# Routing logits from a stationary gate matrix, in pieces per batch, and Sinkhorn column sums set apart

## The chip, the cores and the metric

The program runs on one core of one Trainium2 chip. The metric is the device time of one execution in microseconds, the median of several runs. The engines are named as in the profile: PE is TensorE's matmul, PEld its weight load, DVE is VectorE, ACT is ScalarE, POOL is GpSimd and SP is SyncE, which here only issues DMAs.

## What is computed

Three stages follow each other. The weights and the attention inputs are float32.

```
attn = softmax(q @ k.T / 8 + causal mask + min(-(cum_i - cum_j), 0)) @ v     # 4 batches, 8 heads, 576 x 64
x    = elu(attn_tokens @ w_in) @ w_out                                       # 2304 x 512, 512 -> 2048 -> 512
logits = x @ w_gate                                                          # 2304 x 8
P = exp(logits - logits.max())
for _ in range(8):
    P /= P.sum(1, keepdims=True) + 1e-09
    P /= P.sum(0, keepdims=True) + 1e-09
    P *= N / E                                                               # N = 2304, E = 8
out = sum over e of P[:, e:e+1] * (relu(x @ w1[e]) @ w2[e])                  # 512 -> 1024 -> 512 for 8 experts
```

The change concerns the line with `w_gate` and the loop that normalizes P.

## The kernel before, in words

The first phase does attention and the first feed-forward stage together. Attention works on jobs of two heads: S tiles hold the scores (PE, L302), POOL makes the bias tiles R from the running sums (L273, L276), DVE adds them (L321), ACT takes the exponential (L329), POOL scales the rows (L337), PE transposes them (T, L364 to L370), ACT and DVE copy the transposes, and PE multiplies by V (X, L431). The feed-forward stage has groups of twelve matmuls: `m` groups (L677) for the first layer and `n` groups (L709) for the second. A weight decode for it runs on ACT and DVE (L614 to L634) from tiles `st` that SP loads (L581). The running sums come to `cum` tiles by SP's DMAs (L239), which copy a row to 64 partitions. Batch by batch the feed-forward result lies in `acc`, transposed: 128 of the 512 features on the partitions, four such quarters d, 576 tokens along the row.

When the eight pieces of a batch's `acc` are done, `gate(b)` (L776) makes its logits. It takes 128 tokens of one quarter d of `acc` as the stationary operand and the 128x8 quarter of the gate matrix as the moving one, and adds up four d in PSUM. A batch has four whole blocks of 128 tokens and one of 64, so these are 20 matmuls; a float32 matmul is two instructions in the trace, a pass each, so the trace has 40 for a batch. Two DVE copies (L797, L799) put the logits into `P_t`, a tile of 128 x 18 x 8.

The second phase is the mixture of experts, with `product` (L1006; banks A, B and C, L1023: seven products of six matmuls for each step) and `m2_l2` (L1078; `b`, L1092: twelve matmuls). While its first steps run, the Sinkhorn loop is fitted in: `max_t` and `max_b` bring the global maximum to all partitions, `rows()` divides by the row sums and leaves partial column sums in `small` (L833 to L837), and `cols(it)` multiplies these by a matrix of ones on PE (`col`, L844), after which DVE divides by them (L848 to L850) and calls `rows()` again. There are eight such rounds, and `m2_l2` of the second unit needs the result.

What sets the order: the Python code keeps a model clock `flow` (class `_Flow`, L50). Work for PE is emitted by `flow.pe(cost, fn)`, and what follows it on the other engines by `flow.after(dt, fn)`. `extras()` (L886) is called after each group of the second phase and emits the next Sinkhorn matmul if its input has been emitted. The sequence so emitted is the priority by which the framework's scheduler then lays each engine's instructions in a line, so an edit of one operation can move others. Each engine then runs its own line strictly in that order; PE alone loads the weights of later matmuls ahead. The gate's matrix `wg` is loaded at the start (L1145), the first POOL work are memsets and `make_identity` (L1147 to L1158).

## Time and profile before

| | us |
|---|---|
| runs shown | 2206.74, 2211.27, 2213.0 |
| their median | 2211.27 |
| the profiled execution's own time | 2213.01 |
| its span in the profile | 2211.2 |
| PE busy (share of the span) | 2151.1 (97%) |
| PEld busy | 1901.1 (86%) |
| DVE busy | 1294.1 (59%) |
| ACT busy | 940.2 (43%) |
| POOL busy | 823.3 (37%) |

Busy PE does not mean PE at its peak: matmuls overlap, and the clock granted to TensorE can stand at one of two levels, 1.2 or 2.4 GHz. The profile gives it as a share (PEclk): 1.00 is 2.4 GHz and 0.50 is 1.2 GHz. In the 40 slices of the span, PE is busy nine tenths or more in all but the first three, and PEclk is nine tenths or more in all but the first two, each slice a mean over 55 us.

### The profile page before, as it was taken

Reading aid. Unit: us, or ns where it says so; the run is one execution under the profiler, and the core shown is the slowest. Engines: PE = TensorE matmul, PEld = TensorE weight load, DVE = VectorE, ACT = ScalarE, POOL = GpSimd, SP = SyncE. Lnnn points to the kernel's source line nnn. Section 1 sums busy time; section 2 is a strip of 40 time slices with the busy share of each in tenths; the row PEclk is TensorE's granted clock in tenths of the full one; section 3 lists DMA queues with packets and bytes.
Section 4 is the critical chain, followed back from the end, with each engine's and each line's share of the span. In section 5 each row is a group of like instructions: output and inputs, shape, how many; then the busy total and the mean of one; then the engine's idle time right before and its main releaser. Section 6 shows DMA issues by size and latency. Waiting matters only on the chain.

```text
span 2211.2 us, 33504 instructions
## 1 busy us (share of the span) xinstructions
PE 2151.1 (97%) x12236; PEld 1901.1 (86%) x12236; DVE 1294.1 (59%) x2921; ACT 940.2 (43%) x2201; POOL 823.3 (37%) x1046
## 2 busy tenths in 40 slices
PE   6789999999999999999999999999999999999999
PEld 3357988999998898989998989989899899899898
DVE  5678698555756755555555555555555455555554
ACT  3565545343433444344434444343434443443432
POOL 5676343232402343333333343433333333434330
PEclk8899999999999999999999999999999999999999
DMA  6454444243562421222215221222115221222121
GB/s 198 154 167 169 145 169 159 79 131 106 188 229 96 150 77 59 66 77 67 67 58 195 77 77 58 67 68 76 65 60 195 77 70 56 76 67 77 58 67 38
DMA packets 102227, 228.55 MB, mean 103 GB/s; under 512 B 8816, under 2 KB 24688, under 8 KB 102064
## 3 DMA queue, kind: packets, MB, share of 16 engines
q1 hardware_dynamic: 97456, 209.65, 28.9%
q10 hardware_dynamic: 4608, 16.78, 1.9%
q8 instruction: 96, 1.57, 0.3%
q14 instruction: 67, 0.55, 0.1%
HBM read 189.10 MB, written 37.30 MB: 102 GB/s over the span
## 4 chain that ended last, share of the span: by engine, by line
PE 88%; DVE 5%; POOL 2%; DMA 1%; ACT 1%; issue 1%; SPq 0%; POOLq 0%; DVEq 0%; ACTq 0%
PE b L1092 36%; PE A L1023 18%; PE C L1023 9%; PE n L709 7%; PE m L677 7%; PE B L1023 5%; PE S L302 2%; PE X L431 2%; PE T L364 1%; PE gate L789 1%; DVE R L321 1%; POOL R L273 1%; DVE h L692 0%; DMA xr<-x_d 0%; DVE r L689 0%
## 5 line engine op out<-in xcount | busy, mean ns | idle before, releaser
L1092 PE MATMUL b<-w,h 128*128 128x512 f32 x3456 | 844.7, 393 | 0.0
L1092 PEld LDWEIGHTS b<-w,h 128*128 128x128 f32 x3456 | 645.5, 188 | 125.1
L906 POOL TENSOR_TENSOR w1c<-S,w1c 128x512 fp32r<-128x512 f32 x192 | 263.6, 1395 | 860.6 <-ACT w1c L905 860.6
L1023 PE MATMUL A<-xc,w1c 128*128 128x384 f32 x2304 | 449.5, 336 | 0.0
L1106 DVE SCALAR_TENSOR_TENSOR acc<-b,P_t,acc 128x512 f32<-128x512 f32 x264 | 197.5, 748 | 423.1 <-PE b L1092 423.1
L1023 PEld LDWEIGHTS A<-xc,w1c 128*128 128x128 f32 x2304 | 406.3, 188 | 7.8
L1036 ACT ACTIVATE h<-pre_P 128x384 fp32r<-128x384 f32 x288 | 151.4, 526 | 437.6 <-DVE pre_P L1049 437.3
L677 PE MATMUL m<-xT,w 128*128 128x288 f32 (+2 forms) x1536 | 231.3, 305 | 2.9 <-DVE r L689 1.5
L1023 PE MATMUL C<-xc,w1c 128*128 128x384 f32 x1152 | 233.9, 337 | 0.0
L709 PE MATMUL n<-h,w 128*128 128x288 f32 (+2 forms) x1536 | 222.3, 299 | 3.3 <-DVE r L689 1.6
L677 PEld LDWEIGHTS m<-xT,w 128*128 128x128 f32 x1536 | 214.2, 194 | 12.4 <-issue 5.0
L709 PEld LDWEIGHTS n<-h,w 128*128 128x128 f32 x1536 | 207.3, 188 | 17.3 <-issue 11.1
L1023 PEld LDWEIGHTS C<-xc,w1c 128*128 128x128 f32 x1152 | 206.0, 189 | 7.5
L906 DVE TENSOR_TENSOR w<-sw,w 128x512 fp32r<-128x512 f32 x192 | 155.5, 831 | 59.9 <-ACT w L905 59.9
L1039 DVE SCALAR_TENSOR_TENSOR h<-pre_P,h 128x384 fp32r<-128x384 f32 x288 | 160.8, 558 | 12.3 <-ACT h L1036 0.5
L273 POOL TENSOR_SCALAR R<-cum,cum_m 128x256 f32<-128x256 f32 (+4 forms) x144 | 101.8, 707 | 155.5 <-PE T L370 90.6
L337 POOL TENSOR_SCALAR R<-R,sm 128x64 f32<-128x64 f32 (+8 forms) x144 | 92.5, 650 | 118.6 <-DVE sm L334 64.0
L1036 ACT ACTIVATE h<-A 128x384 fp32r<-128x384 f32 x96 | 47.2, 491 | 192.8 <-PE A L1023 192.8
L905 ACT CAST w<-sw 128x512 fp32r<-128x512 f32 x192 | 109.4, 619 | 21.5 <-PE n L709 16.8
L1057 ACT COPY pre_P<-A 128x384 f32<-128x384 f32 x192 | 92.4, 481 | 60.1 <-PE A L1023 60.1
L1023 PE MATMUL B<-xc,w1c 128*128 128x384 f32 x576 | 117.5, 339 | 0.0
L1023 PEld LDWEIGHTS B<-xc,w1c 128*128 128x128 f32 x576 | 104.6, 190 | 7.8 <-issue 0.2
(162 smaller groups left out, 2288.2 us busy)
## 6 DMA issues: line engine op xcount, KB each, us to landing
sw<-in_w_dram SPq DMA_DIRECT2D x192, 512.0 KB, 3.3
w<-w_sc SPq DMA_DIRECT2D x56, 512.0 KB, 3.6
w_sc<-w ACTq DMA_DIRECT2D x32, 512.0 KB, 3.3
xc_d<-xs SPq DMA_DIRECT2D x28, 384.0 KB, 3.2
xc<-xc_d SPq DMA_DIRECT2D x14, 768.0 KB, 6.0
QK<-in_qk_dram SPq DMA_DIRECT2D x16, 576.0 KB, 5.1
st<-in_wi_dram SPq DMA_DIRECT2D x16, 512.0 KB, 4.5
st<-in_wo_dram SPq DMA_DIRECT2D x16, 512.0 KB, 4.0
```

The costliest lines, as they stand in the source:

```text
L273: nc.gpsimd.tensor_scalar(out=t[:, 0:w], in0=ct[j].rearrange("p w k -> p (w k)")[:, S * z : S * z + w], scalar1=8.0, scalar2=cum_m[:, z, m ...
L337: nc.gpsimd.tensor_scalar(out=R[:, 0:keys], in0=R[:, 0:keys], scalar1=sm[:, 5:6], scalar2=1.0, op0=ALU.mult, op1=ALU.mult)
L677: nc.tensor.matmul(ps[:, 0:n], t[:, a, d * P : (d + 1) * P], x[:, z, d, c0 : c0 + n], start=(d == 0 and o == 0), stop=(d == 3 and o == 2))
L709: nc.tensor.matmul(ps[:, 0:n], t[:, a, f * P : (f + 1) * P], h[:, z, c0 : c0 + n], start=(f == 0 and o == 0), stop=(f == 3 and o == 2))
L905: nc.scalar.copy(hi, x)
L906: eng.tensor_tensor(out=lo, in0=x, in1=f32(hi), op=ALU.subtract)
L1023: nc.tensor.matmul(ps, t[:, a, wi_, kt * P : (kt + 1) * P], x[:, z, kt], start=(first and kt == 0 and o == 0), stop=(kt == 1 and o == 2), ...
L1036: nc.scalar.activation(h[:, 0], src, AF.Relu)
L1039: nc.vector.scalar_tensor_tensor(out=h[:, 1], in0=src, scalar=0.0, in1=f32(h)[:, 0], op0=ALU.max, op1=ALU.subtract)
L1057: nc.scalar.copy(new(name), ps)
L1092: nc.tensor.matmul(ps, h[:, z, c0 : c0 + P], t[:, a, :], start=(f == 0 and o == 0), stop=(f == 3 and o == 2))
L1106: nc.vector.scalar_tensor_tensor(out=a, in0=ps, scalar=q, in1=a, op0=ALU.mult, op1=ALU.add)
```

## The change

The gate turns its operands round. The gate matrix, padded with zeros from 8 to 32 columns, becomes the stationary operand, and 256 or 320 tokens of `acc` stream past it. Quarter d of the features writes its 8 partial logits to PSUM partitions 32d and up, so four matmuls fill four column quarters of the array. ACT copies the 128 rows to the tile `lt`. A second product, `gate_sum`, has 128 tokens of `lt` as the stationary operand and the matrix `sel` (eight columns, which add rows 0 to 7 of the four quarters) as the moving one. A batch goes in two pieces, 256 and 320 tokens or the other way round; each piece is emitted one group of the loop after the other. POOL makes `sel` out of the identity and clears `wg` at the start; the load of `wg` moves behind the first weight load. Finally `rows()` notes a time, model clock plus 3.0, before which `extras()` emits no further column sum. Lines from 149 on are two higher in the changed file, and from the gate on some 22 to 32 higher.

```diff
--- before.py
+++ after.py
@@ -109,6 +109,7 @@
     RA = 9
     NR, NQK, NCB, NSCAN, NA_T, NH = 5, 2, 2, 1, 1, 5
     NX = 3
+    SINKGAP = 3.0
 
 
 
@@ -148,7 +149,8 @@
         "rs": cst.tile([P, 18], F32, tag="rs", name="rs"),
         "cs": cst.tile([P, E], F32, tag="cs", name="cs"),
         "small": cst.tile([P, 16], F32, tag="small", name="small"),
-        "wg": cst.tile([P, 4, E], F32, tag="wg", name="wg"),
+        "wg": cst.tile([P, 4, 32], F32, tag="wg", name="wg"),
+        "sel": cst.tile([P, E], F32, tag="sel", name="sel"),
     }
 
 
@@ -725,7 +727,7 @@
                 nc.sync.dma_start(x2_d[:, d, t0 : t0 + n], a)
                 x2[b] = x2.get(b, 0) + 1
                 if x2[b] == 8:
-                    gates.append(b)
+                    gates.append((gate, b, 0))
 
             flow.after(12 * _mm(n) + 0.05, ev)
         return fn
@@ -774,31 +776,50 @@
     last_g = {k: max(g for g in range(GA) if groups[g][3][1] == k) for k in range(NCHUNK)}
 
 
-    def gate(b):
-
+
+
+    def gate(b, z):
         x, wg_t = accs[b], phc["wg"]
-        ps = ps_s.tile([P, 512], F32, tag="S", name=f"gate{b}")
-        parts, t0 = [], b * S
-        while t0 < (b + 1) * S:
+        cut = [0, 256 + 64 * (b % 2), S]
+        c0, n = cut[z], cut[z + 1] - cut[z]
+        lt = mo1.tile([P, 320], F32, tag="lt", name=f"lt{b}_{z}", bufs=1)
+        ps = ps_s.tile([P, 512], F32, tag="S", name=f"gate{b}_{z}")
+        for d in range(4):
+            nc.tensor.matmul(ps[32 * d : 32 * d + 32, 0:n], wg_t[:, d, :], x[:, d, c0 : c0 + n],
+                             start=True, stop=True)
+
+        def ev():
+            nc.scalar.copy(lt[:, 0:n], ps[:, 0:n])
+            gates.append((gate_sum, b, z, lt, c0, n))
+
+        flow.after(1.1, ev)
+
+    def gate_sum(b, z, lt, c0, n):
+        ps = ps_s.tile([P, 512], F32, tag="S", name=f"gs{b}_{z}")
+        parts, t0 = [], b * S + c0
+        while t0 < b * S + c0 + n:
             r0 = t0 % P
-            n = min(P - r0, (b + 1) * S - t0)
-            parts.append((t0 // P, r0, n, t0 - b * S))
-            t0 += n
-        for i, (tt, r0, n, c0) in enumerate(parts):
-            for d in range(4):
-                nc.tensor.matmul(ps[r0 : r0 + n, 8 * i : 8 * i + 8], x[:, d, c0 : c0 + n], wg_t[:, d, :],
-                                 start=(d == 0), stop=(d == 3))
+            m = min(P - r0, b * S + c0 + n - t0)
+            parts.append((t0 // P, r0, m, t0 - b * S - c0))
+            t0 += m
+        for i, (tt, r0, m, at) in enumerate(parts):
+            nc.tensor.matmul(ps[r0 : r0 + m, 8 * i : 8 * i + 8], lt[:, at : at + m], phc["sel"],
+                             start=True, stop=True)
+        if z == 0:
+            gates.append((gate, b, 1))
         whole = [i for i, x in enumerate(parts) if x[2] == P]
-        half = next(i for i, x in enumerate(parts) if x[2] < P)
+        half = [i for i, x in enumerate(parts) if x[2] < P]
 
         def ev():
             L = phc["P"]
-            i, tt = whole[0], parts[whole[0]][0]
-            nc.vector.tensor_copy(L[:, tt : tt + 4, :], ps[:, 8 * i : 8 * i + 32].rearrange("p (t e) -> p t e", t=4))
-            tt, r0, n, _ = parts[half]
-            nc.vector.tensor_copy(L[r0 : r0 + n, tt, :], ps[r0 : r0 + n, 8 * half : 8 * half + 8])
-            phc["logits"] = phc.get("logits", 0) + 1
-        flow.after(0.2, ev)
+            i, tt, k = whole[0], parts[whole[0]][0], len(whole)
+            nc.vector.tensor_copy(L[:, tt : tt + k, :],
+                                  ps[:, 8 * i : 8 * i + 8 * k].rearrange("p (t e) -> p t e", t=k))
+            for i in half:
+                tt, r0, m, _ = parts[i]
+                nc.vector.tensor_copy(L[r0 : r0 + m, tt, :], ps[r0 : r0 + m, 8 * i : 8 * i + 8])
+            phc["logits"] = phc.get("logits", 0) + z
+        flow.after(0.8, ev)
 
     def logits():
         L, small = phc["P"], phc["small"]
@@ -836,6 +857,7 @@
         nc.vector.tensor_tensor(out=L, in0=L, in1=rs.unsqueeze(2).to_broadcast([P, 18, E]), op=ALU.mult)
         nc.vector.tensor_reduce(out=small[:, 8:16], in_=L.rearrange("p t e -> p e t"), axis=AX.X, op=ALU.add)
         phc["step"] += 1
+        phc["due"] = flow.now + SINKGAP
 
     def cols(it):
         def fn():
@@ -862,7 +884,7 @@
     extra += [(lambda it=it: phc.get("step") == 3 + it, 0.1, cols(it)) for it in range(SINK)]
 
     def extras(force=False):
-        while extra and (force or extra[0][0]()):
+        while extra and (force or (extra[0][0]() and flow.now >= phc.get("due", 0.0))):
             ready, cost, fn = extra.pop(0)
             flow.until(ready)
             flow.pe(cost, fn)
@@ -1142,9 +1164,9 @@
         "r (m z q) -> r m z q", z=2, q=64)
     nc.sync.dma_start(s_raw, s)
     qk_load(0)
-    nc.sync.dma_start(phc["wg"], wg)
     nc.vector.memset(ones, 1.0)
     make_identity(nc, ident)
+    nc.gpsimd.memset(phc["wg"], 0.0)
     nc.gpsimd.memset(mask, 0.0)
     for z in range(2):
         nc.gpsimd.affine_select(
@@ -1183,12 +1205,22 @@
     for i in set_r[0]:
         r_step(i)
     w_dma()
+    nc.sync.dma_start(phc["wg"][:, :, 0:E], wg)
+    sel = phc["sel"]
+    nc.gpsimd.tensor_tensor(out=sel, in0=ident[:, 0:E], in1=ident[:, 32 : 32 + E], op=ALU.add)
+    for i in (64, 96):
+        nc.gpsimd.tensor_tensor(out=sel, in0=sel, in1=ident[:, i : i + E], op=ALU.add)
 
     def att_wait():
         t = att_next_ready()
         if t > flow.now:
             flow.flush(t)
             flow.now = t
+
+    def gates_run():
+        while gates:
+            fn, *args = gates.pop(0)
+            flow.pe(1.0, lambda: fn(*args))
 
     def att_end(k):
         return apos["n"] > chunk_last[k]
@@ -1236,14 +1268,14 @@
                 s_load()
             if "w" in m2 and g in (m2["w"] + 24, m2["w"] + 32):
                 w1_prep(int(g > m2["w"] + 24), 0.0)
-        while gates:
-            flow.pe(2.5, lambda: gate(gates.pop(0)))
+        gates_run()
         w_advance(g)
         flow.until(lambda: all(w in w_done for w in ws) and x_left[k[1]] == 0)
         flow.pe(cost, fn)
     flow.drain()
     while gates:
-        flow.pe(2.5, lambda: gate(gates.pop(0)))
+        gates_run()
+        flow.drain()
     pools["xp%d" % ((B - 1) % NX)].release()
     pools["mo1"].release()
     pools["dec"].release()
```

The order of the instructions moves at the places below. In each name the letters and the first numbers are the tile's, the last number is a buffer's.

The first is the start, on the queue of SP, which issues the loads, from `cum1` on; `st` are weights for the decode, `cum` the running sums, `V` and `QK` inputs of attention. Before:

```order
L239 DMA cum1_137<-cum_d_95 64x256 x2
L581 DMA st0_169<-in_wi_dram 128x1024
L581 DMA st1_171<-in_wi_dram 128x1024
L239 DMA cum2_185<-cum_d_95 64x256 x2
L210 DMA QK2_207<-in_qk_dram 128x2x256
L239 DMA cum3_234<-cum_d_95 64x256 x2
L210 DMA QK3_272<-in_qk_dram 128x2x256
L239 DMA cum4_330<-cum_d_95 64x576 x2
L581 DMA st2_315<-in_wi_dram 128x1024
L239 DMA cum4_330<-cum_d_95 64x512 x2
```

In the changed kernel:

```order
L583 DMA st0_170<-in_wi_dram 128x1024
L241 DMA cum1_138<-cum_d_95 64x256 x2
L583 DMA st1_172<-in_wi_dram 128x1024
L1208 DMA wg_102<-in_wg_dram 128x4x8
L241 DMA cum2_190<-cum_d_95 64x256 x2
L212 DMA QK2_212<-in_qk_dram 128x2x256
L241 DMA cum3_239<-cum_d_95 64x256 x2
L212 DMA QK3_277<-in_qk_dram 128x2x256
L583 DMA st2_320<-in_wi_dram 128x1024
L241 DMA cum4_335<-cum_d_95 64x576 x2
```

`st0` now stands ahead of `cum1`, and `st2` ahead of both loads of `cum4`. On POOL, in the same stretch, the scalings of R2 and R4 (`sm` is the factor) stood ahead of the bias tiles R8 to R11, which need `cum2`. Before:

```order
L337 TENSOR_SCALAR R0_164<-R0_164,sm1_179 128x128
L337 TENSOR_SCALAR R2_180<-R2_180,sm2_200 128x192
L337 TENSOR_SCALAR R2_180<-R2_180,sm3_201 128x256
L337 TENSOR_SCALAR R4_202<-R4_202,sm4_227 128x64
L337 TENSOR_SCALAR R4_202<-R4_202,sm5_228 128x128
L273 TENSOR_SCALAR R8_267<-cum2_185,cum_m_103 128x128 x2
L276 TENSOR_TENSOR R8_267<-R8_267,mask_104 128x64
L273 TENSOR_SCALAR R10_325<-cum2_185,cum_m_103 128x256
L276 TENSOR_TENSOR R8_267<-R8_267,mask_104 128x64
L273 TENSOR_SCALAR R10_325<-cum2_185,cum_m_103 128x256
L276 TENSOR_TENSOR R10_325<-R10_325,mask_104 128x64 x2
```

In the changed kernel:

```order
L275 TENSOR_SCALAR R8_272<-cum2_190,cum_m_104 128x128 x2
L278 TENSOR_TENSOR R8_272<-R8_272,mask_105 128x64
L275 TENSOR_SCALAR R10_330<-cum2_190,cum_m_104 128x256
L278 TENSOR_TENSOR R8_272<-R8_272,mask_105 128x64
L275 TENSOR_SCALAR R10_330<-cum2_190,cum_m_104 128x256
L278 TENSOR_TENSOR R10_330<-R10_330,mask_105 128x64 x2
L339 TENSOR_SCALAR R2_185<-R2_185,sm2_205 128x192
L339 TENSOR_SCALAR R4_207<-R4_207,sm4_232 128x64
L339 TENSOR_SCALAR R4_207<-R4_207,sm5_233 128x128
L339 TENSOR_SCALAR R2_185<-R2_185,sm3_206 128x256
```

The four scalings have moved behind the six instructions for R8 to R11.

The second place is PE at the first gate, that of batch 0, among the `m` groups of the next batch. Before:

```order
L677 MATMUL m2_13_288_5019<-xT1_1239,w33_4318 128x288 x12
L789 MATMUL gate0_5038<-wg_102,acc0_1424 128x8 x16
L789 MATMUL gate0_5038<-wg_102,acc0_1424 64x8 x4
L677 MATMUL m2_14_0_5066<-xT1_1239,w34_4345 128x288 x12
L677 MATMUL m2_14_288_5081<-xT1_1239,w34_4345 128x288 x12
```

In the changed kernel:

```order
L679 MATMUL m2_13_288_5024<-xT1_1244,w33_4323 128x288 x12
L788 MATMUL gate0_0_5044<-acc0_1429,wg_102 32x256 x4
L679 MATMUL m2_14_0_5054<-xT1_1244,w34_4350 128x288 x12
L679 MATMUL m2_14_288_5070<-xT1_1244,w34_4350 128x288 x12
L806 MATMUL gs0_0_5089<-sel_103,lt0_0_5043 128x8 x2
L788 MATMUL gate0_1_5099<-acc0_1429,wg_102 32x320 x4
L679 MATMUL m2_15_0_5104<-xT1_1244,w35_4428 128x288 x12
L679 MATMUL m2_15_288_5120<-xT1_1244,w35_4428 128x288 x12
```

The one block of 20 has become pieces of 4, 2 + 4 and 3, with two groups of twelve between them; gates 1 and 2 look alike. At the last gate, that of batch 3, there are no `m` groups left, and five matmuls of A (six matmuls make a product) stand between the first piece and its sum.

The third place is PE at the last round of the Sinkhorn loop, `col7`. Before:

```order
L844 MATMUL col6_8629<-small_101,ones_94 128x8
L1092 MATMUL b0_3_8738<-w2_1_1_8470,h1_1_1_8523 128x512 x2
L1023 MATMUL C3_8766<-xc0_3_7189,w1c3_8611 128x384 x6
L1023 MATMUL A3_8725<-xc0_4_7224,w1c3_8611 128x384 x6
L1092 MATMUL b0_4_8784<-w2_0_0_8351,h0_0_1_8419 128x512 x2
L844 MATMUL col7_8668<-small_101,ones_94 128x8
L1092 MATMUL b0_4_8784<-w2_0_0_8351,h0_0_1_8419 128x512
```

In the changed kernel:

```order
L866 MATMUL col6_8760<-small_101,ones_94 128x8
L1045 MATMUL C3_8763<-xc0_3_7195,w1c3_8590 128x384 x3
L1045 MATMUL A3_8719<-xc0_4_7223,w1c3_8590 128x384 x6
L1114 MATMUL b0_4_8788<-w2_0_0_8360,h0_0_1_8432 128x512 x3
L1114 MATMUL b0_4_8788<-w2_0_1_8373,h0_1_1_8422 128x512 x3
L1114 MATMUL b0_4_8788<-w2_1_0_8447,h1_0_1_8536 128x512 x3
L1114 MATMUL b0_4_8788<-w2_1_1_8469,h1_1_1_8512 128x512 x3
L866 MATMUL col7_8805<-small_101,ones_94 128x8
```

`col7` now stands behind all twelve matmuls of `b0_4`.

## Rows read from the trace of the kernel before

**Rows 1.** Windows, two long stretches: time, busy of each engine, PEclk, DMA share, GB/s.

```profile
240.00:560.00 320.00, 317.31 (x2510) 289.65 (x2501) 219.79 (x721) 148.43 (x438) 101.75 (x177) 0.98 0.39 131
750.00:2200.00 1450.00, 1450.00 (x7247) 1306.11 (x7246) 772.94 (x1287) 593.94 (x1218) 510.58 (x542) 1.00 0.23 77
```

**Rows 2.** The chain that ended last, gates 0 and 1: start us, us, what.

```profile
400.82 4.03 PE gate L789 x40
...
435.01 2.21 PE X L431 x20
...
439.88 5.76 PE gate L789 x40
```

**Rows 3.** The same chain at gate 3.

```profile
685.89 2.22 PE gate L789 x22
...
689.21 3.64 PE gate L789 x18
```

**Rows 4.** Windows of slow clock, at gates 0 to 3 and in the Sinkhorn loop.

```profile
404.00:409.00 5.00, 5.00 (x31) 4.96 (x31) 1.40 (x6) 0.86 (x2) 0.00 (x0) 0.66 0.00 0
442.00:450.00 8.00, 8.00 (x41) 8.00 (x42) 1.99 (x8) 1.71 (x4) 0.69 (x1) 0.57 0.03 4
585.00:590.00 5.00, 5.00 (x31) 4.96 (x31) 3.78 (x11) 2.32 (x6) 1.16 (x1) 0.66 0.59 187
688.00:699.00 11.00, 11.00 (x44) 10.35 (x44) 1.57 (x6) 1.19 (x3) 3.33 (x4) 0.53 0.28 87
718.00:723.00 5.00, 4.46 (x17) 4.32 (x17) 4.72 (x15) 1.48 (x3) 0.02 (x1) 0.66 0.62 186
746.00:750.00 4.00, 4.00 (x14) 3.47 (x13) 1.72 (x3) 0.59 (x1) 1.23 (x2) 0.57 0.55 196
```

**Rows 5.** PE's waits from 692 to 800 us: total, times, longest.

```profile
PE col L844 <- DVE small L837: 7.8, 5, 2.9
```

**Rows 6.** Timeline of PE in the Sinkhorn loop: start, us, [idle before, releaser].

```profile
718.54 0.41 PE L844 MATMUL col<-small,ones 128*128 128x8 f32 x2 [2.90 <-DVE small L837]
...
744.61 0.39 PE L844 MATMUL col<-small,ones 128*128 128x8 f32 x2 [2.81 <-DVE small L837]
```

**Rows 7.** Timeline of PE at the start.

```profile
37.18 1.55 PE L431 MATMUL X<-aA,V 128*64 128x256 f32 x8
```

**Rows 8.** Timeline of PEld in one X piece.

```profile
435.26 0.14 PEld L431 LDWEIGHTS X<-aB,V 128*64 128x64 f32 x2
...
435.53 0.14 PEld L431 LDWEIGHTS X<-aB,V 128*64 128x64 f32 x2
```

**Rows 9.** Groups of ACT by line and shape: a copy from PSUM.

```profile
L719 ACT COPY acc<-n 128x320 f32<-128x320 f32 x4 | 1.6, 412 | 0.0
```

**Rows 10.** The chain past the Sinkhorn loop: one product and one `b` group.

```profile
750.03 1.04 PE A L1023 x6
...
752.11 2.77 PE b L1092 x12
```

**Rows 11.** Timeline of SP, ACT, DVE and POOL at the start.

```profile
27.95 1.10 SPq L239 DMA_DIRECT2D cum<-cum_d  x2
29.16 0.52 SPq L581 DMA_DIRECT2D st<-in_wi_dram  x1
...
33.67 0.66 ACT L614 ACTIVATE db<-st 128x512 f32<-128x512 f32 x1 [5.36 <-DMA st<-in_wi_dram]
...
22.92 0.77 DVE L624 SCALAR_TENSOR_TENSOR db<-db,st 128x512 f32<-128x512 f32 x1
...
22.49 1.96 POOL L273 TENSOR_SCALAR R<-cum,cum_m 128x128 f32<-128x128 f32 x2
...
28.01 0.60 POOL L276 TENSOR_TENSOR R<-R,mask 128x64 f32<-128x64 f32 x2
```

**Rows 12.** Windows, two stretches of the first 114 us.

```profile
46.00:64.00 18.00, 14.22 (x94) 8.50 (x98) 11.81 (x43) 8.88 (x27) 10.75 (x18) 0.97 0.58 196
81.00:114.00 33.00, 25.33 (x170) 13.86 (x169) 24.36 (x91) 19.20 (x55) 27.25 (x46) 1.00 0.50 164
```

## The prediction

> **What bounds the kernel now.** I read the windows first, to find where PE is the limit. From 240 to 560 us PE is busy 317.3 of 320 us, and from 750 to 2200 us all the time at full clock [rows 1]. All that the change touches lies before 750 us, so whatever PE saves at a gate or in the Sinkhorn loop reaches the end, unless another engine is late behind it. Then I read the chain of waits at the gates. Gate 0 takes 4.03 us of it for 40 passes and gate 1 takes 5.76 us for the same 40 [rows 2]; gate 3 takes 2.22 + 3.64 = 5.86 us [rows 3]. PE is busy throughout in each, so what differs is the clock, and the windows show it: a gate is followed, and gates 1 and 3 are already accompanied, by a stretch at the lower level, 1.2 GHz [rows 4]. The reader should see that PE counts as fully busy there: only PEclk tells that it does half the work. In the second phase the list of waits has one entry, `col` for `small`, 7.8 us in five waits [rows 5], and the two longest, 2.90 and 2.81 us [rows 6], are each followed by such a slow stretch as well (the windows from 718 and from 746 us). Last, the start: there PE waits for chains through POOL, DVE and ACT, and the mark to watch is the second product with V, at 37.18 us [rows 7].
>
> **The change part by part.** *The passes.* At full clock 40 passes of the old gate take 4.03 us, 0.10 us each, with only 8 columns streaming: the price of a pass is that of its weights. Of this kind the new gate keeps five matmuls for a batch (`gs`), 10 passes: 10 x 0.10 = 1.0 us. New are eight matmuls, 16 passes, with 32 stationary columns and 256 or 320 streamed ones. The nearest row is X, float32 with 64 stationary columns and 320 streamed. Its weights are loaded two at a time every 0.27 us [rows 8], so two passes share 0.27 us for 320 columns, and 256 columns in proportion take 0.21 us. I take the pairing over: eight passes in order, each next to the one before, take four and a half such steps, 1.20 us for 320 and 0.96 us for 256. A batch then costs 1.0 + 1.20 + 0.96 = 3.16 us against 4.03, 0.87 us less, **3.5 us for four batches**. Bounds: no overlap at all makes 8 x (0.27 + 0.21) + 1.0 = 4.8 us for a batch, 0.8 us more than now; all four quarters at once makes 2 x (0.27 + 0.21) + 1.0 = 1.96 us.
>
> The Trainium skill speaks against this part as well as for it. In "TensorEngine Tiling (Array Packing)", section "Tiling Modes", it says that changing the tiling mode drains TensorE; the change adds such switches around each of eight pieces. The X piece answers: 20 passes took 2.21 us [rows 2], and twelve of 320, four of 192 and four of 64 columns at the pair rate make 2.03 us, so getting in and out costs at most 0.2 us. By that bound 16 switches would cost up to 1.6 us, which is within the range.
>
> *The wait for `lt`.* `gs` needs ACT's copy out of PSUM; the nearest copy takes 0.41 us [rows 9], and the handing over to it and from it comes on top, for which no row stands alone. At gates 0 to 2 two groups of twelve matmuls stand between, which hide it; if ACT's own queue were late by over 2 us, that cover would be gone. At gate 3 five matmuls of A stand ahead of the first `gs` (6 take 1.04 us [rows 10]) and three ahead of the second: 0.87 and 0.52 us. The second is hardly more than the copy; I charge **0.5 us** there, and 1 us as the bound. The eight copies themselves, 3.3 us, lie on ACT, which is under half busy. DVE has three copies for a batch where it had two, 0.2 us each beside PE's work.
>
> *The clock.* In the four gate windows 5, 8, 5 and 11 us pass at 0.66, 0.57, 0.66 and 0.53 of full speed [rows 4]. The work lost is 1.7 + 3.4 + 1.7 + 5.2 = 12.0 us. In the new kernel the runs of 8-column passes last 4 or 6 passes, 0.4 to 0.6 us, not 40, and full groups lie between them. X, whose passes use half the columns, runs for 2.21 us from 435.01 us and does not lower the clock: at gate 1 it sinks from 442 us on, two microseconds into the gate. So I take **12.0 us** as returned; bounds 0 and 12.0.
>
> *The Sinkhorn loop.* The gap of 3.0 on the model clock moves the loop on PE less than its name says. Counted in PE's order from `mxb` on, 176 matmuls stood between it and `col7`, leaving out the `col`; now there are 180. Where it counts is the last round: `col6` to `col7` held 12 matmuls of a product and 4 of `b`, now 9 and 12. With 0.174 and 0.231 us each [rows 10] that is 3.0 us of cover before and 4.3 us now, and the wait of 2.81 us there falls by 1.3 us to 1.5. The slow stretch behind it, 4 us at 0.57, is 1.7 us, and I count it as gone with the long wait. The 2.90 us before `col2` stay, as both engines have about the same work up to there (28 matmuls on PE before and after, 16 instructions on DVE). **3.0 us**; bounds 0 and, if every wait and both stretches went, 7.8 + 1.7 + 1.7 = 11.2.
>
> *The start.* POOL's memset and three small additions fall into a time when it waits for the sums anyway, and the load of `wg` is wanted only at 400 us. What counts is the order. ACT stood 5.36 us until 33.67 us for `st2`, with the copies for the second product with V behind it; SP had issued that load at 29.16 us, behind a load of `cum4` which at 27.95 us waited for POOL's bias tiles R8 to R11 [rows 11]. Now `st2` stands ahead of it, held only by the last reader of `st0`, the DVE instruction at 22.92 us. That is worth up to 5.4 us. Against it, on POOL the scalings of R2 go behind R8 to R11, which took from 22.49 to 28.61 us, 6.1 us, so the first product with V is late by up to that. The second product comes after both, and the later work hangs on it. I take **3 us** of gain, a little more than half the ACT stall, with bounds of -6 and +8 (the stall, and 2.6 us because the first long slow stretch, which ends at 46 us, would end that much sooner).
>
> *The sum.* 3.5 - 0.5 + 12.0 + 3.0 + 3.0 = 21.0 us. Against the profiled execution's own time, 2213.0 us, that is 2192.0. The median shown is 1.7 us lower; I put the forecast between the two, at **2191 us**.
>
> **The rivals.** *All four quarters at once.* Then a batch's gate costs 1.96 us, 1.2 less than I took: 4 x 1.2 = 4.8 us, 2186 us. For it: the outputs lie in four disjoint column quarters. Against it: the only row that shows column groups, X, shows pairs. This is what the Trainium skill holds, in "TensorE: Matmul & The Clock Gate", section "Part 3: Packing small matmuls — row/col tiling": tiles in different column groups run side by side, a few nanoseconds apart.
>
> *One quarter after the other.* The change doesn't do what it says: 4.8 us for a batch, 6.7 us more in all than I took, 2198 us. Against it: the pairs of X.
>
> *The clock still falls.* With 32 of 128 columns in use the new gate may leave the clock as the old one did. Then the 12.0 us stay lost, 2203 us. For it: gate 3 meets the first products and the two small products of the maximum, among which the clock stayed low from 688 to 698 us. Against it: X.
>
> *The start loses.* POOL's order decides and not ACT's: -6 instead of +3, 2200 us.
>
> *Slower.* The reordered start keeps PE from the unbroken run after which the clock rose at 46 us. In the two stretches of full clock up to 114 us PE is busy 14.2 + 25.3 us [rows 12]; at half the clock that doubles, and the 11.5 us of idle time there take up some of it: 28 us lost, and the 3 us gained at the start with them, 2222 us. The point from which it makes the kernel slower is 21 + 6.6 = 28 us lost, so nearly all of both stretches must run at the lower level. For it: a wait of 2.9 us is enough to bring the clock down in the Sinkhorn loop. Against it: from 59 us on PE's order is the old one again, and with it the runs that brought the clock back.
>
> **How the numbers follow.** About 0.3%, 6.6 us, is what a measurement of this kernel can tell from no change. Forecast 0.45; four at once 0.20; one after the other 0.10; the clock still falls 0.12; the start loses 0.08; slower 0.05. Below 2204.6 us lie the first two and the third whole, and most of the two cases near 2200 to 2203: faster 0.86. Same 0.09, the rest of those two. Slower 0.05. The range goes from 2179 us (four at once, and the Sinkhorn loop or the start at the better bounds by 7 us) to 2205 us (the clock case and the late start); slower stays outside, with about 0.12 for the ends.
>
> **What would show it.** Gate 0 with `gs` taking about 3.2 us of the chain in place of 4.03, weights of the new gate loading two at a time; PEclk of 1.00 in the windows behind each gate; one wait of some 1.5 us before the last `col`, and near 2.9 us before `col2`; the second product with V ahead of 37 us, and no ACT wait of 5 us for `st`. Wrong would be: a slow stretch behind any gate, `gs` waiting for ACT at gates 0 to 2, or a first phase that reaches gate 0 later than 400.8 us.

## The result and the profile after

| | before | changed |
|---|---|---|
| median of 4 runs (lowest to highest) | 2211.26 us (2206.74 to 2213.0) | 2184.59 us (2180.91 to 2185.1) |
| profiled execution: own time, span | 2213.0, 2211.2 us | 2184.45, 2182.6 us |

The ratio is 0.9879 (95% interval 0.9861 to 0.9897), 26.7 us less, and the spans of the two profiles differ by 28.6 us. Where they come from is seen by taking the same matmul of PE in both traces (the 800th of line `m`, the 61st `b` and so on) and comparing its start:

| mark on PE | before, us | changed, us | lead | gained since the mark above |
|---|---|---|---|---|
| first matmul of gate 0 | 400.7 | 394.3 | 6.4 | 6.4, the start |
| 800th `m` | 439.2 | 429.5 | 9.7 | 3.3, gate 0 |
| 800th `n` | 465.8 | 451.5 | 14.4 | 4.7, gate 1 |
| last `n` | 685.6 | 673.7 | 11.9 | -2.5, gate 2 and behind it |
| 61st `b` | 751.9 | 730.7 | 21.2 | 9.3, gate 3 and Sinkhorn loop |
| end | 2211.2 | 2182.6 | 28.6 | 7.4, the part in which nothing was changed |

The chain of waits of the changed kernel at gates 0 and 1, which answers to [rows 2]:

```profile
394.36 0.57 PE gate L788 x8
394.93 3.39 PE m L679 x24
398.31 0.34 PE gs L806 x4
398.66 0.68 PE gate L788 x8
...
402.93 0.56 PE gs L806 x6
...
430.19 0.68 PE gate L788 x8
430.87 1.93 PE m L679 x13
432.80 0.75 PE gs L806 x6
433.55 0.57 PE gate L788 x8
...
437.48 0.34 PE gs L806 x4
```

Gate 0 is 0.57 + 0.34 + 0.68 + 0.56 = 2.15 us of the chain and gate 1 2.34 us, where they were 4.03 and 5.76. Eight passes of 320 columns take 0.68 us. At gate 1 only 13 `m` stand between the first piece and its sum, where gate 0 has 24, so the two gates are not alike in this; `gs` did not wait there either. The windows of the changed kernel (time, busy PE, PEclk, DMA share, GB/s), four at the gates and two in the Sinkhorn loop, answer to [rows 4]:

```profile
394.00:404.00 10.00, 10.00 (x83) 1.00 0.01 2
430.00:440.00 10.00, 10.00 (x82) 1.00 0.30 96
566.00:586.00 20.00, 16.72 (x125) 1.00 0.64 211
673.00:690.00 17.00, 17.00 (x106) 1.00 0.46 151
718.00:723.00 5.00, 2.81 (x15) 0.96 0.59 204
723.00:728.00 5.00, 5.00 (x19) 0.70 0.31 110
```

In this profile the clock leaves full speed at no gate. At gate 2 that is an exception: of the nine profiles with the new gate, the other eight all have a stretch at the lower level there, which loses 1.7 us of work, behind a wait of PE for the copy to `lt`. This is the window at gate 2 in e9_after, a second profile of the same kernel:

```profile
563.00:583.00 20.00, 17.61 (x124) 0.91 0.69 223
```

From 573 to 575 us the granted clock is 0.50 there, 1.2 GHz. What spared the first profile no run shows; PE waits in it too and is busy only 16.72 of 20 us at gate 2. Its timeline of PE there:

```profile
566.70 0.72 PE L788 MATMUL gate<-acc,wg 128*32 128x256 f32 x8
...
573.66 0.61 PE L806 MATMUL gs<-sel,lt 128*128 128x8 f32 x4 [2.30 <-ACT lt L792]
574.20 0.74 PE L788 MATMUL gate<-acc,wg 128*32 128x320 f32 x8
...
578.86 0.82 PE L806 MATMUL gs<-sel,lt 128*128 128x8 f32 x6 [0.55 <-ACT lt L792]
```

and ACT's, which shows why the copy to `lt` comes 6 us after its gate:

```profile
567.52 0.52 ACT L927 CAST xc<-xr 128x384 fp32r<-128x384 f32 x1 [1.32 <-DMA xr<-x_d]
568.70 0.51 ACT L927 CAST xc<-xr 128x384 fp32r<-128x384 f32 x1 [0.66 <-POOL xr L993]
...
571.28 0.51 ACT L927 CAST xc<-xr 128x384 fp32r<-128x384 f32 x1 [0.78 <-POOL xr L993]
...
573.25 0.35 ACT L792 COPY lt<-gate 128x256 f32<-128x256 f32 x1
```

The copy is itself short. It stands in ACT's queue behind the conversions to `xc` for the second phase, which wait for GpSimd, the first of those shown for a DMA, and behind four instructions of the feed-forward layer that follow them.

The Sinkhorn loop, PE's waits from 660 to 800 us and its timeline, answers to [rows 5, 6]:

```profile
PE col L866 <- DVE small L858: 4.6, 4, 2.2
```

```profile
702.92 0.39 PE L866 MATMUL col<-small,ones 128*128 128x8 f32 x2 [1.86 <-DVE small L858]
...
721.10 0.39 PE L866 MATMUL col<-small,ones 128*128 128x8 f32 x2 [2.19 <-DVE small L858]
...
723.35 4.16 PE L1114 MATMUL b<-w,h 128*128 128x512 f32 x12
727.35 0.28 PE L866 MATMUL col<-small,ones 128*128 128x8 f32 x2
```

7.8 us of waits have become 4.6. The last column sum no longer waits; the one before it now does, and in this profile one stretch of low clock is left behind that wait (twelve `b` in 4.16 us, 2.88 at full clock).

At the start, the timelines of PE and of SP's queue [rows 7, 11]:

```profile
24.04 0.47 PE L366 MATMUL T<-ident,R 128*128 128x128 f32 x1 [5.89 <-POOL R L339]
...
26.17 1.55 PE L433 MATMUL X<-aA,V 128*64 128x256 f32 x8 [0.35 <-ACT aA L382]
...
31.92 0.87 PE L433 MATMUL X<-aA,V 128*64 128x256 f32 x8 [0.17 <-ACT aA L382]
```

```profile
19.24 0.53 SPq L583 DMA_DIRECT2D st<-in_wi_dram  x1
```

`st2` is issued 9.9 us sooner. The first product with V is 4.8 us late, since GpSimd's scalings of R2 now follow the next bias tiles; the second is 5.3 us early. ACT's longest wait for `st` is 1.8 us, where it was 5.36.

Last, the steady part. The groups of PE from 1000 to 1600 us, of the kernel before and then of the changed one (count, busy us, mean ns of one):

```profile
L1092 PE MATMUL b<-w,h 128*128 128x512 f32 x1384 | 337.9, 393 | 0.0
L1023 PE MATMUL A<-xc,w1c 128*128 128x384 f32 x928 | 180.0, 335 | 0.0
```

```profile
L1114 PE MATMUL b<-w,h 128*128 128x512 f32 x1392 | 334.4, 389 | 0.0
L1045 PE MATMUL A<-xc,w1c 128*128 128x384 f32 x924 | 180.7, 336 | 0.0
```

Same code, same order, full clock in both; yet a `b` takes 389 ns in place of 393. From start to start of neighbours (after 800 us, some 3,000 pairs of `b` and 1,850 of `A`) a `b` follows a `b` every 226.7 ns in place of 230.6, and an `A` an `A` every 175.3 in place of 173.7. These spacings are alike in every group: before, the third of a group of twelve is always 235 or 236 ns, the fourth 224 or 225.

### The profile page after: what moved, and what is told of

It reads as the page before. It is cut to its first block, busy times and chain, and to the rows that moved or that the text cites. A ratio compares the mean times of both kernels' runs of the same rounds, so it can differ in the third digit from the quotient of the medians.

```text
span 2182.6 us, 33415 instructions
## 1 busy us (share of the span) xinstructions
PE 2121.1 (97%) x12180; PEld 1883.4 (86%) x12180; DVE 1294.6 (59%) x2925; ACT 941.9 (43%) x2209; POOL 829.9 (38%) x1050
## 4 chain that ended last, share of the span: by engine, by line
PE 87%; DVE 5%; POOL 2%; DMA 1%; issue 1%; ACT 1%; SPq 0%; POOLq 0%; ACTq 0%; DVEq 0%
PE b L1114 36%; PE A L1045 18%; PE C L1045 9%; PE n L711 7%; PE m L679 7%; PE B L1045 5%; PE S L304 2%; PE X L433 2%; PE T L366 1%; POOL R L275 1%; DMA xr<-x_d 1%; DVE R L323 1%; POOL R L339 0%; DVE h L694 0%; DMA xc_d<-xs 0%
## 5 line engine op out<-in xcount | busy, mean ns | idle before, releaser
L1114 PE MATMUL b<-w,h 128*128 128x512 f32 x3456 | 830.7, 389 | 0.0
L679 PEld LDWEIGHTS m<-xT,w 128*128 128x128 f32 x1536 | 209.3, 190 | 15.5 <-issue 5.7
L1061 DVE SCALAR_TENSOR_TENSOR h<-pre_P,h 128x384 fp32r<-128x384 f32 x288 | 161.2, 560 | 11.5
L927 ACT CAST w1c<-S 128x512 fp32r<-128x512 f32 x192 | 110.4, 627 | 0.0
```

The lines of the kernel that those rows point to most:

```text
L679: nc.tensor.matmul(ps[:, 0:n], t[:, a, d * P : (d + 1) * P], x[:, z, d, c0 : c0 + n], start=(d == 0 and o == 0), stop=(d == 3 and o == 2))
L927: nc.scalar.copy(hi, x)
L1061: nc.vector.scalar_tensor_tensor(out=h[:, 1], in0=src, scalar=0.0, in1=f32(h)[:, 0], op0=ALU.max, op1=ALU.subtract)
L1114: nc.tensor.matmul(ps, h[:, z, c0 : c0 + P], t[:, a, :], start=(f == 0 and o == 0), stop=(f == 3 and o == 2))
```

## The experiments

The first four build the change up from the kernel before, one part at a time, on one chip. The kernel before took 2209.21 us there (median of 23, 2203.65 to 2215.35).

**e1_pad**: an unused tile shifts `w`, `h`, `pre` and `acc` by as much as `wg` and `sel` do.

```diff
+        "pad": cst.tile([P, 104], F32, tag="pad", name="pad"),
```

> The kernel before with one more constant tile of 416 bytes a partition that nothing reads; no instruction moves. It stands for the 384 + 32 bytes by which the change's wg and sel shift w, h and acc in SBUF. Reading that it tests: in the steady part the matmuls b follow each other every 226.7 ns after the change and every 230.6 ns before, A every 175.3 against 173.7, which together make the 7.4 us that the change gains after 730 us. Theory (it is the place of the tiles): b at about 226.7 ns, A at about 175.3 ns, and 7.4 us less, 2204 us. Rival (it hangs on the instruction stream or on what ran before): b stays at 230.6 ns and the time at 2211 us.

Measured: 2203.52 us (12 runs, 2198.16 to 2211.43), ratio 0.998 (0.9967 to 0.9994); `b` every 226.7 ns, `A` every 175.3. PE's groups from 1000 to 1600 us:

```profile
L1093 PE MATMUL b<-w,h 128*128 128x512 f32 x1392 | 334.4, 389 | 0.0
```

It is the place of the tiles: 5.7 us by the medians (by the interval 1.3 to 7.3), and from the 61st `b` to the end 7.4 us in the profile, all of that row of the table. This part hardly differs between executions: from the 200th `b` to the end, the kernel before and e3_gap take 1401.1 us, and the changed kernel and every run with its places 1394.0.

**e2_start**: e1_pad's shift by the real tiles, and the new start (memset, later load, the additions to `sel`), with the old gate.

```diff
-    nc.sync.dma_start(phc["wg"], wg)
+    nc.gpsimd.memset(phc["wg"], 0.0)
...
     w_dma()
+    nc.sync.dma_start(phc["wg"][:, :, 0:E], wg)
...
```

> The kernel before with the change's edits at the start alone (wg as a tile of 32 columns and sel, the memset, the later load, the additions), so that the start's order and the tiles' places are those of the change; the old gate of 40 passes and no gap in the Sinkhorn loop. Theory: gate 0 begins at 394.4 us in place of 400.8 (6.4 us), gates 0 and 1 still take 4.0 and 5.8 us with slow stretches behind them, and with the 7.4 us of the tiles' places the time is 2197.5 us. Forecast's own term for the start, 3 us, would give 2201 us with the places and 2208 us without. Rival (the start's gain is lost again by the gates): gate 0 at 394.4 but not over 3 us left by gate 3.

Measured: 2194.74 us (5 runs), ratio 0.9946 (0.9929 to 0.9963), 8.8 us below e1_pad (the two intervals leave some 3 to 12 us); gate 0 begins at 391.5 us. The gain stays: the last `n` is 9.0 us ahead of the kernel before. Its windows at gates 0 to 3 show the old clock, at gate 3 a milder one than in [rows 4]; together they lose 1.7 + 3.4 + 1.7 + 1.7 = 8.5 us of work, where [rows 4] have 12.0:

```profile
391.00:400.00 9.00, 9.00 (x67) 0.81 0.01 2
429.00:440.00 11.00, 11.00 (x70) 0.69 0.13 38
571.00:581.00 10.00, 9.69 (x71) 0.83 0.51 161
676.00:690.00 14.00, 14.00 (x89) 0.88 0.44 141
```

The edit moves SP's order and POOL's at once, so what each is worth alone is not shown.

**e4_nogap**: the changed kernel less the gap, that is e2_start with the new gate.

```diff
-        phc["due"] = flow.now + SINKGAP
```

> The changed kernel without the gap. In PE's order only the last column sum moves, seven matmuls b (7 x 0.227 = 1.6 us) earlier. Forecast's term for the gap, 3.0 us, would give 2187.6 us. Rival (in the changed kernel the gap does nearly nothing, since the gate's new pieces have moved the loop already): col7 waits up to 1.6 us, and the time is between 2184.6 and 2186.2 us.

Measured: 2182.45 us (4 runs), ratio 0.989 (0.9872 to 0.9908). The gate is thus worth 12.3 us. By the marks of the two profiles it gains 8.0 us over gates 0 and 1, loses 1.8 over gate 2, and gains 5.5 over gate 3 and the loop up to the 200th `b`. `col7` waits 0.29 us, and the other waits are those of the changed kernel. Without the gap the time is not longer: in the changed kernel the gap has no effect that these runs can tell.

**e3_gap**: the gap alone, in the kernel before.

```diff
+        phc["due"] = flow.now + 3.0
...
-        while extra and (force or extra[0][0]()):
+        while extra and (force or (extra[0][0]() and flow.now >= phc.get("due", 0.0))):
```

> The kernel before with the gap of 3.0 in the Sinkhorn loop alone. Forecast: its 3.0 us for the Sinkhorn part, from the wait before the last column sum and the slow stretch behind it: 2208 us. Rival: the gap alone moves what the loop waits for, not how long; the waits of col stay near 7.8 us in all with their two slow stretches, and the time within 1 us of 2211.

Measured: 2206.62 us (12 runs), ratio 0.9989 (0.9977 to 1.0): 2.6 us, near the forecast's 3.0 and on the edge of what can be told. Here the waits do fall, from 7.8 to 4.3 us, against the rival. The gap and the gate's new pieces both take most of the wait before `col7`, 2.81 us before, 1.01 with the gap alone and 0.29 with the gate alone, so whoever comes second finds little left there.

The next four went together (before: 2209.18 us, 11 runs).

**e5_serial**: e4_nogap with all four parts in one column quarter.

```diff
-            nc.tensor.matmul(ps[32 * d : 32 * d + 32, 0:n], wg_t[:, d, :], x[:, d, c0 : c0 + n],
-                             start=True, stop=True)
+            nc.tensor.matmul(ps[0:32, 0:n], wg_t[:, d, :], x[:, d, c0 : c0 + n],
+                             start=(d == 0), stop=(d == 3))
```

> The changed kernel without the gap (e4_nogap, 2182.5 us) and with all four parts of a gate's sum in the same column quarter, added up there by accumulation; the selection product then reads 32 rows. Same number of passes, same columns streamed. Theory (in the changed kernel the four quarters run side by side, so eight passes take 0.67 us for 320 columns and 0.57 us for 256): in one quarter each pass takes what a pair of X takes, 0.27 and 0.21 us, so a batch's two pieces take 2.1 + 1.7 us, 2.6 us more, and four batches 10.4 us: 2193 us. Forecast (quarters in pairs): 1.2 and 0.96 us would have been the side-by-side price, and the difference 1.7 us a batch, 6.6 us: 2189 us. Rival (the pieces are short because 32 columns of weights are, not because quarters run side by side): 0.67 and 0.57 us stay, 2182 us.

Measured: 2193.15 us (6 runs), ratio 0.9929 (0.9912 to 0.9945), 10.7 us above e4_nogap. Its timeline of PE at gate 0:

```profile
389.22 1.91 PE L788 MATMUL gate<-acc,wg 128*32 128x256 f32 x8
...
394.97 2.34 PE L788 MATMUL gate<-acc,wg 128*32 128x320 f32 x8
```

The same eight passes take 1.91 and 2.34 us in one quarter and 0.57 and 0.68 us of the chain in four. Side by side it is. (This run also adds up in PSUM, but so does the old gate, at 0.10 us a pass.) This is what the Trainium skill says in "TensorE: Matmul & The Clock Gate", section "Part 3: Packing small matmuls — row/col tiling", and the trace agrees.

**e6_split**: e2_start with the old gate's passes in five pieces of eight, one behind each group of products.

```diff
+        if z + 1 < len(parts):
+            gates.append((b, z + 1, ps))
+            return
```

> e2_start (the old gate, 2194.7 us) with the old gate's 40 passes given out as five pieces of eight, one after each group of products, into the same tile; the same passes, nothing else. [...] Rival (what keeps the clock in the changed kernel is the streamed 256 and 320 columns, and any five pieces of 8-column passes lower it): granted clock near 0.8 over each gate as in e2_start, 2193 to 2196 us.

Measured: 2191.84 us (6 runs), ratio 0.9924 (0.9907 to 0.9941), 2.9 us below e2_start. Its windows at gates 0 to 3:

```profile
392.00:404.00 12.00, 12.00 (x100) 1.00 0.01 1
425.00:445.00 20.00, 19.96 (x166) 1.00 0.38 125
565.00:590.00 25.00, 23.58 (x178) 1.00 0.68 225
672.00:690.00 18.00, 18.00 (x115) 0.91 0.42 139
```

The mechanism holds: the old passes keep full clock at gates 0 to 2 once products stand between them, and the lead over e2_start grows by 1.6 us over gate 0 and 3.2 us over gate 1. Behind gate 2 PE waits for DVE (the longest time 2.06 us) and 1.0 us of that is lost again. At gate 3 no products were left to stand between: the passes came out as 22 and 18 in a row, as in the old kernel, so nothing was tried there, and nothing was gained. The record had put the case in which the clock stays full at 2183 to 2188 us; that was not reached.

**e7_dve2**: the copy to `lt` of batch 2 on DVE.

```diff
-            nc.scalar.copy(lt[:, 0:n], ps[:, 0:n])
+            (nc.vector.tensor_copy if b == 2 else nc.scalar.copy)(lt[:, 0:n], ps[:, 0:n])
```

> The changed kernel with the copies to lt of batch 2 alone on VectorE in place of ScalarE. At gate 2 ScalarE's copy stood behind conversions to xc, each of which waited for GpSimd, and PE waited 2.30 + 0.55 us for it. Theory: those 2.9 us go, gate 2 ends that much sooner: 2181.7 us; if the waits for acc at 594 to 604 us (2.5 us) hang on them as well, 2179 us. Rival (VectorE's own queue holds the subtractions that wait for the same conversions, so its copy comes no sooner, or the evictions behind it are late instead): a wait of over 2 us stays and the time is 2184 to 2186 us.

Measured: 2182.13 us (4 runs), ratio 0.9878 (0.986 to 0.9897). The rival holds for the first copy, as PE's timeline shows:

```profile
573.65 0.61 PE L806 MATMUL gs<-sel,lt 128*128 128x8 f32 x4 [2.94 <-DVE lt L792]
...
574.87 4.98 PE L679 MATMUL m<-xT,w 128*128 128x288 f32 x24
```

DVE's subtractions to `xc` wait for the same conversions, and the copy behind them starts at 573.18 us. The second wait, of 0.55 us, is gone, and 24 `m` behind the first take 4.98 us in place of 3.44; but neither is the copy's doing, for e9_after, with the copy on ACT, has the same:

```profile
570.36 0.61 PE L806 MATMUL gs<-sel,lt 128*128 128x8 f32 x4 [2.29 <-ACT lt L792]
...
571.58 4.98 PE L679 MATMUL m<-xT,w 128*128 128x288 f32 x24
```

There the 24 `m` run largely at the lower clock level and the second sum does not wait. Moving the copy to DVE thus made the first wait 0.65 us longer and changed nothing else that can be told; the whole time, 0.5 us from that of e9_after, decides nothing. Gate 2's loss is the chain of `xc`, not the engine that copies.

**e8_gap5**: a gap of 4.5.

```diff
-    SINKGAP = 3.0
+    SINKGAP = 4.5
```

> The changed kernel with a gap of 4.5 in place of 3.0 in the Sinkhorn loop. In PE's order the work between column sums becomes 5.4, 5.4, 5.7, 3.5, 5.9, 5.9, 5.9 and 5.7 us in place of 5.4, 5.2, 5.5, 2.9, 3.4, 3.9, 4.0 and 4.3 us (a product's matmul 0.1745 us, a b 0.227 us). Theory (too little cover is what PE's 4.6 us of waits for the sums hang on, and the stretch of low clock behind the longest): waits of 1 us or less in all, full clock, 4 to 6 us less: 2179 to 2181 us. Rival (VectorE is late for other work, or the later end of the loop holds up the second expert's sums): same waits in other places, 2184 to 2186 us.

Measured: 2179.25 us (4 runs, 2177.22 to 2182.69), ratio 0.9869 (0.9846 to 0.9892). PE's waits from 660 to 800 us:

```profile
PE col L866 <- DVE small L858: 4.3, 3, 2.1
```

The waits are hardly shorter, but between 680 and 760 us PEclk is 1.00, where the changed kernel shows 0.98. From the last `n` to the 200th `b` it takes 112.5 us, 2.3 less than the changed kernel. The next three kernels with this gap bear it out: 112.8 to 114.0 us there and no low clock in the loop, against 114.8 to 116.5 us and one or two slow stretches in the three profiles with the gap of 3.0. So the longer gap gives back the clock, not the waits. By the whole time the two can't be told apart: e9_after, the changed kernel again, has a ratio of 0.9863.

The last four also went together (before: 2211.64 us, 9 runs).

**e9_after**: the changed kernel, no edit.

> The changed kernel once more, beside the next three on the same chip, as the base for the gap and for one more look at how far the start differs between executions. Theory: the time of the first measurement, 2184.6 us, within 2 us; gate 0 anywhere from 388 to 398 us, since the seven profiles with this start reach gate 0 between 389.2 and 397.4 us. Rival (the start is the same each time): gate 0 at 394.3 us.

Measured: 2181.6 us (4 runs, 2180.1 to 2182.2), ratio 0.9863 (0.985 to 0.9877); gate 0 at 391.1 us. That is 3 us below the first measurement, so medians of different groups of runs are not to be compared closer than that. The start is not the same each time, though its instructions are. Three profiles with the old order reach gate 0 at 395.7, 400.7 and 404.3 us, mean 400.2; the eleven with the new order lie between 389.2 and 397.4 us, mean 392.5. What is seen to differ within an order is the clock: from 40 to 80 us it is 0.71 in the kernel before and 0.96 in e1_pad. By these means the orders lie 7.7 us apart, though two of the three old ones also have the tiles' old places.

**e10_pad32, e11_pad64, e12_pad96**: e8_gap5 with 32, 64 or 96 unused bytes more.

```diff
+        "pad": cst.tile([P, 8], F32, tag="pad", name="pad"),
```

(`[P, 16]` and `[P, 24]` in the other two.)

> The changed kernel with the gap of 4.5 (e8_gap5, 2179.3 us) and an unused tile of 32 bytes behind sel: w, h, pre and acc lie 448 bytes further on than in the kernel before, in place of 416. Theory 1 (what counts is where a tile stands within 128 bytes; before it was 0, the change made it 32, here it is 64): a value of its own for the matmuls b, A, B and C, as yet unknown, the same in every group. Theory 2 (any place but that of before is good): b at 226.7 and A at 175.3 ns, 2179 us.

> As the one before, with 64 bytes: 480 further on than in the kernel before, 96 within 128 bytes, which is where xc and w1c stand, that the change does not move. Theory 1: again a value of its own. Theory 2: b at 226.7 and A at 175.3 ns, 2179 us.

> As the one before, with 96 bytes: 512 further on than in the kernel before, so that every tile stands where it stood within 128 and within 512 bytes. Theory 1 (the place within 128 or 512 bytes decides): b back at 230.6 ns, A at 173.7 ns, and the 7.4 us of the steady part lost again: 2186.7 us. Theory 2 (any other place is good): b at 226.7 ns, 2179 us.

Measured, with the kernels that have 0 and 32:

| place of `w` and `h` within 128 bytes | `b` to `b`, ns | `A` to `A`, ns | 200th `b` to the end, us | median, us |
|---|---|---|---|---|
| 0: before, e12_pad96 | 230.6, 230.6 | 173.7, 173.7 | 1401.1, 1401.1 | -, 2186.03 |
| 32: changed, e8_gap5 | 226.7, 226.7 | 175.3, 175.3 | 1394.0, 1394.0 | 2184.59, 2179.25 |
| 64: e10_pad32 | 230.9 | 173.3 | 1402.9 | 2191.9 |
| 96: e11_pad64 | 228.8 | 174.8 | 1402.9 | 2190.35 |

The gap of 4.5 is in all of these but the kernel before and the changed one. The medians also hold the start, which differs between executions; the fourth column does not. The places are worked out from the order and sizes of the tiles in the kernel; a profile shows no address.

Theory 1 holds: at 0 again, 512 bytes further on, the spacings of the kernel before come back, and the 7 us with them. Whether the place counts within 128 or within 512 bytes these runs do not tell. Of the four places the change hit the best by chance. PE's groups from 1000 to 1600 us in e12_pad96:

```profile
L1115 PE MATMUL b<-w,h 128*128 128x512 f32 x1384 | 337.9, 393 | 0.0
L1046 PE MATMUL A<-xc,w1c 128*128 128x384 f32 x922 | 178.9, 335 | 0.0
```

## Why the prediction was right, and where it was not

The forecast was 2191 us, its range 2179 to 2205; 2184.6 us came out, faster as said. By parts, measured as differences of medians: place of the tiles 5.7, start 8.8, gate 12.3, gap none that can be told; 26.8 together, with the changed kernel less its gap at the end. The forecast had 0, 3.0, 15.0 (3.5 - 0.5 + 12.0) and 3.0, 21 together. So the total is near, and its parts are less so: the places and the start gave 11.5 us more than forecast, the gate and the gap 5.7 us less. That these partly cancel is luck. Two of the prediction's own signs of being wrong came up at gate 2: `gs` waited for ACT, and in eight of nine profiles a slow stretch followed.

- *The passes* (3.5 us). "I take the pairing over" failed: four quarters run at once, as in the first rival, and a batch at gates 0 and 1 costs 2.15 and 2.34 us, not 3.16. X shows pairs because it has only two column groups of 64 to run side by side; the row could not tell two from four. e5_serial settles it. At some 1.8 us a batch, the term is about 7 us. The eight weight loads of a piece lie within 0.16 us in the profile, not two every 0.27. Two steps of 0.27 us would be 0.54 for a piece of 320 columns; by that rate of X getting in and out costs at most the 0.14 us above it.
- *The wait for `lt`* (0.5 us). "At gates 0 to 2 two groups of twelve matmuls stand between, which hide it" failed at gate 2, for the reason that the same sentence names as its condition: ACT's queue was late. It cost 2.30 + 0.55 us there (once, 2.3 us, in the other profiles of this gate with ACT's copy, with the slow stretch behind it), and nothing at gate 3, where 0.5 was charged. At gate 1 the first cover was 13 matmuls and not 24, and was enough.
- *The clock* (12.0 us). The mechanism is right for gates 0, 1 and 3, where every profile with the new gate has 1.00, and e6_split brings the clock back at gates 0 to 2 without the new gate. The size is what failed, twice. 12.0 us were read from one profile; the other three with the old gate in one block lose 10.2 (e1_pad), 8.5 (e2_start) and 8.5 us (e3_gap) at the gates. And at gate 2 a slow stretch behind the wait for the copy to `lt` takes 1.7 us again in eight of nine profiles. Against e2_start some 6.8 us came back. Over gate 2 as a whole nothing was gained. So the whole gate, with cheaper passes, gave 12.3 us and not 15.0.
- *The Sinkhorn loop* (3.0 us). The wait of 2.81 us before `col7` went, to 0 and not to 1.5, and the 2.90 before `col2` became 1.86. But the step "counted in PE's order" took the order of the change for the gap's doing. Most of it is the gate's: without the gap only `col7` moves, by seven `b`. Alone, in the kernel before, the gap is worth 2.6 us; what failed is adding it to a gate that takes the same wait. And a wait that was not foreseen came up before `col6`, 2.19 us with a slow stretch of its own; what makes DVE late there was not tried. In the profile, gate 3 and the loop gave 9.3 us; some 3 of that also show in e1_pad and e2_start, where neither was changed, so that part is low clock that this one profile of before had there and others had not.
- *The start* (3.0 us). The direction and the mechanism held: late first product, early second. "A little more than half the ACT stall" was too little: the profile shows 6.4 us, the medians 8.8. Why it is more stays open; the three profiles with the old order alone lie 8.6 us apart at gate 0, so no single one could size this term.
- *Not in the sum at all*: where tiles stand in SBUF. A shift of 416 bytes was read in the diff as a matter of size alone. Those 5.7 us (7.4 in the profile) are a term put at nothing, and about as large as the 6.4 us between forecast and result.

The slower rival did not come. In the two stretches of [rows 12] the clock of the changed kernel is lower in this profile:

```profile
46.00:64.00 18.00, 13.10 (x75) 0.81 0.56 195
...
81.00:114.00 33.00, 26.98 (x159) 0.86 0.46 160
```

0.81 and 0.86 are far from the lower level throughout that the rival needed, and the first 46 us are at 0.96 where they were at 0.82. The other profiles do not tie the first of these to the order: from 46 to 64 us they have 0.81 to 0.97 with the new one, and e3_gap, with the old one, has 0.81. From 81 to 114 us it is 0.84 to 0.95 with the new order and 0.95 to 1.00 with the old.

## What to carry to other kernels

A short gate or router product costs PE its passes and its clock: stream the many columns over few weights, in as many column quarters as there are partial sums, and put other products between the pieces. Before a copy is called hidden, read what stands ahead of it in its engine's queue and what that waits for; moving it to another engine helps only if that engine does not wait for the same chain. When a change adds or grows any tile, compare the spacing of the unchanged matmuls in the steady part of both profiles first, and read a slow stretch or a term of the start in more than one profile; here the spacing gave a fifth to a quarter of the gain, and an unused tile of the right size would have given it alone.

## What the runs showed that was not expected

The spacing of matmuls depends on where tiles begin, within 128 or 512 bytes, in four values for four places: 224 to 236 ns from one place in a group of twelve to the next in the kernel before, and 225 to 228 in the changed one. `A`, whose own operands `xc` and `w1c` did not move, changes with it (173.3 to 175.3 ns), so it is not only the reading of a matmul's own tiles. The Trainium skill ("SBUF — State Buffer", section "Who interferes with whom") says that among the engines only the pair of ports that VectorE and GpSimd share is contended for and that PE waits for nobody; by that alone a shift of 32 bytes would not be expected to change PE's pace. Here it does. Whether PE waits for another engine in this or is slower by itself no run shows, so what meets what stays open.

The clock at the start differs between executions of the same order, and with it the time at which gate 0 is reached, by over 8 us in either order. A term of a few microseconds there can't be read from one profile.
